# Two halves of a matmul array pass projection groups in two different orders of each triple, 6 turns apart in place of 18

## The chip, the cores and the metric

The kernel runs on one core of a Trainium2 chip. The metric is device time in microseconds (us) from the first to the last work of the core, as the median over runs. The engines of the core work side by side, each on its own list of instructions in order, and wait for one another by semaphores: TensorE (PE, matrix multiplications into PSUM, the accumulator memory of eight banks), VectorE (DVE), ScalarE (ACT), GpSimd (POOL) and SyncE (SP, which here issues every DMA). Times of instructions come from one profiled execution.

## The reference

The output mixes two branches on the same input x (2048 rows of 512) by a gate of one number per row:

```python
g = sigmoid((x * gate_w).sum(-1, keepdims=True))
a = A_ref(x, wqkv, wo)     # 32 heads of 16, causal, window of 256 keys, then @ wo
b = (sigmoid(x @ w_gate) * (x @ w_up)) @ w_down     # F = 1376
return g * a + (1 - g) * b
```

Everything is float32. The kernel makes the products of the projections from a high and a low part of each operand, three products for one: high by high, high by low, low by high.

## The kernel before

**Stages.** A first stage (to about 72 us) projects some q, k and v. Then a loop over steps `u` (`for u in range(N)`, L732; N = 140) runs the attention and, between its pieces, the remaining projections. A last stage multiplies by `w_down` and `wo` and writes the output.

**The attention in the loop.** A step `u` is one group of four heads and one block of 128 rows (8 groups of 16 blocks, 128 steps). Each step has four sub-steps `hh`, one for a head. In each, `s_part(u, hh)` (L305) makes a block of scores on TensorE and DVE takes its row maximum; `st_part(u - LAG, hh ^ 1)` (L353) makes the transposed scores of the step nine earlier, with the maximum built in, and ACT takes the exponent. Both kinds have two PSUM buffers (`"s"` and `"st"`), so a score waits for the maximum, and a transposed score for the exponent, two sub-steps back. After the four heads, POOL masks the block (`mask_p`, L368). At each even `u` TensorE multiplies two masked blocks with v (`pv_part`, L385), and ACT copies the result later (`o_take`, L405). From u=128 (`NU`) there are no scores left, from u=137 no transposed scores.

**Two halves of the array.** Scores and their transposes contract over 64 rows, so a score in the upper half of the array's rows runs beside a transposed score in the lower half. The projections contract over 128 rows and are cut in two to fit in: a *group* is one accumulation of 12 products (`k3 = 3 * ND`) into one PSUM bank; each product is done once by the lower half of the rows (`half` 0) and once by the upper half (`half` 1), both adding into the same bank. Groups are of three kinds: `proj_mm` (q and k, L251; tile `pj`), `gu_mm` (gate and up, L475; tile `gu`), `tail_mm` (the last columns of gate and up, with the gate of the rows, L514; tile `tp`). All three take their banks from tag `"misc"`, which has three, in turn.

**Turns.** `turns()` (L612) is the order of all groups of the loop, `n_rest` = 111 of them: 72 gate/up, 26 projections and 13 of the 16 tails. In turn `t` the lower half does product `t` of the list, the upper half product `t - SHIFT`; with SHIFT = 18 the upper half is a group and a half behind, and always in another bank. A call of `next(slots)` does three turns (`GAP`). The loop calls it after each sub-step: three or four times in a step up to u=127 (the last sub-step of an odd `u` has none), and from u=128 twice after `hh` 1 and twice after `hh` 3. The list of work is `rest` in order of f, then gate or up, then row chunk c; projections are put in `work` at given steps (L765 to L773) and go first.

**What follows a group.** When the upper half has ended a group, its evacuation is put at the head of `acts`; each sub-step takes one entry from `behind` and one from `acts` (L792 to L795), ahead of its turns. For a gate/up group ACT copies the bank to a tile `sp` (four buffers) and the store is issued at the next step (`later`). For a projection ACT copies it (`proj_raw`), then makes the high part (`proj_hi`), and DVE subtracts for the low part (`proj_lo`); at each eighth step `stack_build` (L275) sends two finished projections to the ring that scores read, three DMAs a step. For a tail DVE transposes the bank and copies a column (`tail_post`, L523). When the last row chunk of a gate/up weight is done, `gu_next` (L487) puts the split of the next weight in the same tile.

**The loop's end.** Three tails are held back (`HOLD`): one runs at u=138 with all 128 rows ahead of the last `pv_part`, the other two behind the loop (`hold_group`, L716).

Of the kernel before, what the change touches and what calls it, by code (L numbers as in the profile page):

```python
# [17 lines left out]
ND = D // P  # L18
# [5 lines left out]
NC = T // CH  # L24
NB = T // P
# [3 lines left out]
NFM = NF - 2  # L29
# [9 lines left out]
LAG = 9  # L39
# [2 lines left out]
QB = 32  # L42
HOLD = 3
GAP = 3
SHIFT = 18
TAIL = 109
TREAD = 136
WD_LOAD = {119: 0, 120: 1, 122: 2, 123: 3, 127: 4, 128: 5, 130: 6, 131: 7, 133: 8, 134: 9, 135: 10}
# [7 lines left out]
def gated_mix_kernel(  # L56
# [47 lines left out]
    NSTEP = NG * NC  # L104
# [24 lines left out]
    with ExitStack() as actx:  # L129
# [27 lines left out]
        wq = {}  # L157
# [81 lines left out]
        pj = {}  # L239
# [1 line left out]
        parts = {}  # L241
        stg = {}

        def group_mm(pt, wh, wl, c, k, half):
            d, w = divmod(k, 2) if k < 2 * ND else (k - 2 * ND, 2)
            r = slice(0, P) if half is None else slice(64 * half, 64 * half + 64)
            mm(pt, (wl if w == 2 else wh)[r, d], (xl if w == 1 else xh)[r, d, c * CH:(c + 1) * CH],  # L247
               start=k == 0 and half != 1, stop=k == 3 * ND - 1 and half != 0,
               skip_group_check=half is not None)

        def proj_mm(s, k, half=None):  # L251
            g, c = divmod(s, NC)
            if s not in pj:
                pj[s] = ps.tile([P, CH], F32, tag="misc", name=f"pj{s}", bufs=3)
            group_mm(pj[s], *wq[g], c, k, half)

        def proj_raw(s):
            raws[s] = cpool.tile([P, CH], F32, tag="sp", name=f"pr{s}", bufs=4)
            nc.scalar.copy(raws[s], pj[s])
            pj[s] = raws.pop(s)  # L260

        def proj_hi(s):
            if s % 2 == 0:
                stg[s // 2] = (
                    cpool.tile([P, CH2], F32R, tag="hb", name=f"sh{s}", bufs=4),
                    cpool.tile([P, CH2], F32R, tag="hb", name=f"sl{s}", bufs=4),
                )
# [114 lines left out]
        acts = []  # L382
# [74 lines left out]
        def load_gu(f, w):  # L457
            raw_gu[f, w] = cpool.tile([P, D], F32, tag="draw", name=f"guraw{f}_{w}", bufs=2)
            nc.sync.dma_start(raw_gu[f, w], wgu[f, w])

        gv = w0.rearrange("p l (w d f) -> p l w d f", w=2, d=ND)

        def split_gu(f, w):
            raw = raw_gu.pop((f, w)).rearrange("p (d f) -> p d f", d=ND)
            hi, lo = gv[:, 0, w], gv[:, 1, w]

            def first_half():
                nc.scalar.copy(hi, raw)
                behind.append(lambda: nc.vector.tensor_tensor(lo, raw, hi.bitcast(F32), op=ALU.subtract))

            acts.append(first_half)

        gp = {}

        def gu_mm(f, c, w, k, half=None):  # L475
            if (f, c, w) not in gp:
                gp[f, c, w] = ps.tile([P, CH], F32, tag="misc", name=f"gu{f}_{c}_{w}", bufs=3)
            group_mm(gp[f, c, w], gv[:, 0, w], gv[:, 1, w], c, k, half)

        def gu_post(f, c, w):  # L480
            t = cpool.tile([P, CH], F32, tag="sp", name=f"sp{f}_{c}_{w}", bufs=4)
            nc.scalar.copy(t, gp.pop((f, c, w)))
            later.append((gu_d[w, f, :, c * CH:(c + 1) * CH], t))
            if f + 1 < NFM and c == 0:
                load_gu(f + 1, w)

        def gu_next(f, c, w):  # L487
            if f + 1 < NFM and c == NC - 1:
                split_gu(f + 1, w)

        tw = []
# [19 lines left out]
            nc.scalar.copy(hi, raw)  # L511
            behind.append(lambda: nc.vector.tensor_tensor(lo, raw, hi.bitcast(F32), op=ALU.subtract))

        def tail_mm(b, k, half=None):  # L514
# [4 lines left out]
            mm(tp[b][:, 0:TW], (xl if w == 1 else xh)[r, d, b * P:(b + 1) * P], tw[d][int(w == 2)][r, 0:TW],  # L519
               start=k == 0 and half != 1, stop=k == 3 * ND - 1 and half != 0,  # L520
               skip_group_check=half is not None)

        def tail_post(b):  # L523
            t = cpool.tile([P, CH], F32, tag="sp", name=f"tt{b}", bufs=4)
            nc.vector.transpose(t[:, 0:2 * TF], tp[b][:, 0:2 * TF])
            nc.vector.tensor_copy(gsum[:, b:b + 1], tp.pop(b)[:, 2 * TF:2 * TF + 1])
            later.append((tail_d[b], t[:, 0:2 * TF]))
# [38 lines left out]
        def proj_slot(s, k, half):  # L566
            g, c = divmod(s, NC)
            d, w = divmod(k, 2) if k < 2 * ND else (k - 2 * ND, 2)
            r = slice(64 * half, 64 * half + 64)
            mm(pair_of_banks(f"ph{s}")[half], wq[g][int(w == 2)][r, d], (xl if w == 1 else xh)[r, d, c * CH:(c + 1) * CH],  # L570
               start=k == 0, stop=k == 3 * ND - 1)

        def proj_sum(s):
            lower, upper = halves.pop(f"ph{s}")
            t = cpool.tile([P, CH], F32, tag="sp", name=f"psum{s}", bufs=4)
            nc.scalar.copy(t, lower)
            pj[s] = t
            behind.append(lambda: nc.vector.tensor_tensor(t, upper, t, op=ALU.add))
            soon.append(lambda: proj_post(s))
# [3 lines left out]
        ]  # L583
        rest = [
            (
                lambda k, h=None, a=(f, c, w): gu_mm(*a, k, h),
                lambda a=(f, c, w): gu_next(*a),
                lambda a=(f, c, w): gu_post(*a),
            )
            for f in range(NFM) for w in range(2) for c in range(NC)  # L590
        ] + [
            (lambda k, h=None, b=b: tail_mm(b, k, h), lambda: None, lambda b=b: tail_post(b)) for b in range(NB)
        ]
        work = []
        going = []

        def proj_group(s):
            return lambda k, h=None: proj_mm(s, k, h), lambda: None, lambda: proj_out(s)

        def run_first(n):  # L600
            for _ in range(n):
# [10 lines left out]
        def turns():  # L612
            k3 = 3 * ND
            groups = []
            for t in range(n_rest * k3 + SHIFT):
                if t and t % GAP == 0:
                    yield
                if t % k3 == 0 and len(groups) < n_rest:
                    groups.append((work or rest).pop(0))
                for half, v in enumerate((t, t - SHIFT)):  # L620
                    if 0 <= v < n_rest * k3:
                        groups[v // k3][0](v % k3, half)
                if t >= SHIFT and (t - SHIFT) % k3 == k3 - 1:
                    _, after, post = groups[(t - SHIFT) // k3]
                    acts.insert(0, lambda after=after, post=post: (post(), after()))

        def slot(h, d, c):
            return (xh, xl)[h][:, d, c * CH:(c + 1) * CH]
# [93 lines left out]
        n_rest = len(rest) + NSTEP - 6 - HOLD  # L722
        N = NU + PVLAG + 1
        SUMS = NU - 13 + PVLAG + 1
        U_LAST = 4 * (NSTEP - 2 - 5)
        HLOAD = N - 2 * AHEAD
        done = 0
        slots = turns()
        sdma = []
        wo_raw = []  # L730

        for u in range(N):  # L732
            if u == LAG:
                vctx.close()
# [26 lines left out]
            if u == WO:  # L761
                both = apool.tile([P, ND, CH], F32, tag="w0", name="woraw")
                wo_raw.extend(both[:, d] for d in range(ND))
                nc.sync.dma_start(both, wo.rearrange("(c p) n -> p c n", p=P))
            s4 = {5: 5, 9: 6, U_LAST: NSTEP - 2, U_LAST + 1: NSTEP - 1}.get(u)  # L765
            if u % 4 == 3 and u > LAG and (u + 2) // 4 + 4 < NSTEP - 2:
                s4 = (u + 2) // 4 + 4
            if s4 is not None:
                if u < LAG:
                    first.insert(0, (  # L770
                        lambda k, h, s4=s4: proj_slot(s4, k, h), lambda s4=s4: proj_sum(s4)))
                else:
                    work.append(proj_group(s4))  # L773
# [113 lines left out]
        for n, (c, f) in enumerate(steps):  # L887
# [42 lines left out]
            for t in range(4):  # L930
                b = 4 * c + t
# [60 lines left out]
```

## Time and profile before

| | us |
|---|---|
| median of 3 runs | 745.94 (745.91 to 746.12) |
| span of the profiled execution | 743.8 |
| TensorE busy in it | 737.1 |
| DVE, ACT, POOL busy | 504.5, 432.3, 171.7 |
| loop's first turns / last lone turns | from 72.0 / to 567.3 |

A row of a timeline has the start in us from the span's start, the duration in us, the engine, the line, the operation, output and inputs by the program's names, partitions by columns, and a count where equal rows are merged; in brackets stands idle time of the engine just before, and what ended it. Matmuls are pipelined: the next one starts before the last one has ended, so the cost of one in a row is the distance of the starts. Two rows with nearly the same start are the two halves of the array at work together, and so is a row with the count x2.

### The profile page before, as it was taken

How to read it: one execution, taken by the hardware profiler on the slowest of the kernel's cores; microseconds unless marked ns; L12 is line 12 of the kernel's file. 1: busy time of each engine (PE TensorE's matmuls, PEld its weight loads, DVE VectorE, ACT ScalarE, POOL GpSimd, SP SyncE). 2: the span in 40 equal slices, each digit the busy share in tenths (PEclk: the TensorE clock that was granted, in tenths of full speed). 3: DMA queues.
4: the chain of work that ended last, by engine and by line, in shares of the span. 5: the costliest groups of instructions: out<-in, count | busy, mean ns of one | idle time of the engine just before them, and what ended most of it. 6: DMA issues, size and time to landing. Idle time of an engine off the chain costs nothing.

```text
span 743.8 us, 17724 instructions
## 1 busy us (share of the span) xinstructions
PE 737.1 (99%) x6310; PEld 585.2 (79%) x6310; DVE 504.5 (68%) x1518; ACT 432.3 (58%) x921; POOL 171.7 (23%) x256
## 2 busy tenths in 40 slices
PE   8999999999999999999999999999999999999997
PEld 7888777887777877778787787778777878787886
DVE  5368767766776766776677676677745685848573
ACT  6423676666676667666667666766655573625341
POOL 7000333233233233323323333232331000000000
PEclk9999999999999999999999999999999999999999
DMA  8341434435434453443543426553367878869561
GB/s 302 102 115 34 103 97 118 127 91 160 125 103 119 120 152 109 120 113 110 153 117 99 126 69 174 151 144 116 92 239 206 233 190 212 196 169 227 148 136 58
DMA packets 94321, 103.66 MB, mean 139 GB/s; under 512 B 44926, under 2 KB 57214, under 8 KB 94232
## 3 DMA queue, kind: packets, MB, share of 16 engines
q1 hardware_dynamic: 94232, 102.53, 49.9%
q8 instruction: 49, 0.80, 0.5%
q14 instruction: 40, 0.33, 0.2%
HBM read 45.32 MB, written 31.99 MB: 104 GB/s over the span
## 4 chain that ended last, share of the span: by engine, by line
PE 97%; DVE 1%; DMA 1%; issue 0%; ACT 0%; SPq 0%; POOL 0%; DVEq 0%; POOLq 0%
PE gu L247 28%; PE pv L394 12%; PE pj L247 11%; PE s L315 7%; PE st L361 5%; PE tp L519 5%; PE pd L78 5%; PE pd L80 5%; PE pd L79 5%; PE vh L556 3%; PE pa L78 2%; PE pa L79 2%; PE pa L80 2%; PE vps L79 1%; PE vps L78 1%; PE vps L80 1%
## 5 line engine op out<-in xcount | busy, mean ns | idle before, releaser
L321 DVE CUSTOM_DVE_ANT_0 junk<-s,mask 128x384 f32<-128x384 f32 (+2 forms) x512 | 271.8, 531 | 126.3 <-PE s L315 69.7
L366 ACT ACTIVATE pt<-st 128x384 f32<-128x384 f32 (+2 forms) x512 | 241.6, 474 | 169.9 <-PE st L361 65.3
L247 PE MATMUL gu<-xh,w 64*128 64x512 f32 x1152 | 295.1, 392 | 0.0
L247 PE MATMUL gu<-xl,w 64*128 64x512 f32 x576 | 190.5, 392 | 0.0
L371 POOL TENSOR_SCALAR_AFFINE_SELECT pt<-pt 128x512 f32<-128x512 f32 x128 | 87.7, 685 | 377.2 <-ACT pt L366 377.2
L247 PEld LDWEIGHTS gu<-xh,w 64*128 64x128 f32 x1152 | 160.6, 184 | 14.1
L361 PE MATMUL st<-ring 64*128 64x384 f32 (+2 forms) x536 | 170.1, 332 | 0.2 <-ACT pt L366 0.2
L315 PE MATMUL s<-ring 64*128 64x384 f32 (+2 forms) x536 | 166.6, 329 | 0.4 <-DVE mx L321 0.4
L315 PEld LDWEIGHTS s<-ring 64*128 64x128 f32 x536 | 95.3, 184 | 37.3 <-DVE nm L331 12.5
L361 PEld LDWEIGHTS st<-ring 64*128 64x128 f32 x536 | 97.0, 184 | 11.2 <-issue 2.7
L247 PEld LDWEIGHTS gu<-xl,w 64*128 64x128 f32 x576 | 90.6, 185 | 3.8
L394 PE MATMUL pv<-pt,V 128*32 128x384 f32 (+2 forms) x1408 | 91.0, 388 | 0.0
L247 PE MATMUL pj<-xh,wqh 64*128 64x512 f32 (+1 forms) x228 | 88.6, 395 | 0.4 <-ACT xh L74 0.4
L247 PE MATMUL pj<-xl,wqh 64*128 64x512 f32 (+1 forms) x228 | 88.2, 393 | 0.2 <-DVE xl L75 0.2
L376 POOL TENSOR_SCALAR_AFFINE_SELECT pt<-pt 128x512 f32<-128x512 f32 x112 | 74.4, 664 | 0.0
L247 PE MATMUL pj<-xh,wql 64*128 64x512 f32 (+1 forms) x228 | 69.9, 392 | 0.0
L394 PEld LDWEIGHTS pv<-pt,V 128*32 128x32 f32 x1408 | 37.2, 109 | 35.6 <-issue 29.5
L78 PE MATMUL pd<-ring,hb 128*128 128x512 f32 x160 | 63.0, 394 | 0.0
L80 PE MATMUL pd<-ring,hb 128*128 128x512 f32 x160 | 62.8, 392 | 0.0
L79 PE MATMUL pd<-ring,hb 128*128 128x512 f32 x160 | 62.3, 390 | 0.0
L74 ACT CAST hb<-V 128x512 fp32r<-128x512 f32 x40 | 24.9, 623 | 53.0 <-DVE V L700 51.3
L247 PEld LDWEIGHTS pj<-xh,wqh 64*128 64x128 f32 (+1 forms) x228 | 41.7, 185 | 3.4 <-ACT xh L74 0.9
(122 smaller groups left out, 1145.0 us busy)
## 6 DMA issues: line engine op xcount, KB each, us to landing
gu_scratch<-sp SPq DMA_DIRECT2D x72, 256.0 KB
V<-gu_scratch SPq DMA_DIRECT2D x36, 512.0 KB
ring<-sh SPq DMA_DIRECT2D x128, 128.0 KB
ring<-sl SPq DMA_DIRECT2D x64, 128.0 KB
guraw<-in_wgu_dram SPq DMA_DIRECT2D x18, 256.0 KB
V<-in_xT_dram SPq DMA_DIRECT2D x16, 256.0 KB
oT_scratch<-ob SPq DMA_DIRECT2D x128, 32.0 KB
xl<-oT_scratch SPq DMA_DIRECT2D x16, 256.0 KB
```

The costliest lines, as they stand in the source:

```text
L78: mm(ps, lh, rh, start=first, stop=False)
L79: mm(ps, lh, rl, start=False, stop=False)
L80: mm(ps, ll, rh, start=False, stop=last)
L247: mm(pt, (wl if w == 2 else wh)[r, d], (xl if w == 1 else xh)[r, d, c * CH:(c + 1) * CH], start=k == 0 and half != 1, stop=k == 3 * ND - 1 ...
L315: mm(pt[:, (k - k0) * P:(e - k0) * P], lhsT, blk(g, k, hh, 1, e - k), start=k == k0, stop=e == i + 1, skip_group_check=True,)
L321: nc.vector.tensor_tensor_reduce(junk[:, 0:n], pt[:, 0:n], mask[:, 3 * P - n:], scale=1.0, scalar=NEG, op0=ALU.add, op1=ALU.max, accum_out ...
L361: mm(pt[:, (q - j) * P:(e - j) * P], lhsT, blk(g, q, hh, 0, e - q), start=q == j, stop=e == last, skip_group_check=True,)
L366: nc.scalar.activation(pts[u][:, hh, 0:n], pt[:, 0:n], AF.Exp, scale=SCALE)
L371: nc.gpsimd.affine_select(p[:, :, 0:P], p[:, :, 0:P], pattern=[[0, HG], [1, P]], compare_op=ALU.is_ge, fill=0.0, base=0, channel_multiplie ...
L376: nc.gpsimd.affine_select(p[:, :, 2 * P:], p[:, :, 2 * P:], pattern=[[0, HG], [-1, P]], compare_op=ALU.is_gt, fill=0.0, base=0, channel_mu ...
L394: mm(pv[32 * hh:32 * hh + 32, (q % 4) * P:(q % 4 + e - q) * P], V[:, j, h * VW:h * VW + 32], p[:, hh, (q - j) * P:(e - j) * P], start=Fals ...
L519: mm(tp[b][:, 0:TW], (xl if w == 1 else xh)[r, d, b * P:(b + 1) * P], tw[d][int(w == 2)][r, 0:TW], start=k == 0 and half != 1, stop=k == 3 ...
```

## The change

The upper half goes 6 turns behind the lower one. So that the halves still never work on the same group in the same turn, groups are taken three at a time and the halves pass each triple in different orders: the lower half 0, 2, 1 and the upper half 1, 0, 2 (`TURN`). Which half opens a bank (`start`) and which one closes it (`stop`) now depends on which comes second, and a group's evacuation is queued when both halves have ended it. Since work is taken in threes, projections are put in the list at other steps (`proj_at`), often two at a time. `gu_next` counts a weight's groups instead of looking at c.

```diff
-SHIFT = 18
+SHIFT = 6
+TURN = ((0, 2, 1), (1, 0, 2))
...
-        def group_mm(pt, wh, wl, c, k, half):
+        def group_mm(pt, wh, wl, c, k, half, second):
...
-               start=k == 0 and half != 1, stop=k == 3 * ND - 1 and half != 0,
+               start=k == 0 and not second, stop=k == 3 * ND - 1 and (half is None or second),
...
+        gu_left = {}
+
         def gu_next(f, c, w):
-            if f + 1 < NFM and c == NC - 1:
+            gu_left[f, w] = gu_left.get((f, w), NC) - 1
+            if f + 1 < NFM and gu_left[f, w] == 0:
                 split_gu(f + 1, w)
...
             groups = []
+            halves_done = {}
             for t in range(n_rest * k3 + SHIFT):
                 if t and t % GAP == 0:
                     yield
-                if t % k3 == 0 and len(groups) < n_rest:
-                    groups.append((work or rest).pop(0))
+                if t % (3 * k3) == 0 and len(groups) < n_rest:
+                    groups.extend((work or rest).pop(0) for _ in range(3))
                 for half, v in enumerate((t, t - SHIFT)):
                     if 0 <= v < n_rest * k3:
-                        groups[v // k3][0](v % k3, half)
-                if t >= SHIFT and (t - SHIFT) % k3 == k3 - 1:
-                    _, after, post = groups[(t - SHIFT) // k3]
-                    acts.insert(0, lambda after=after, post=post: (post(), after()))
+                        n, k = divmod(v, k3)
+                        n += TURN[half][n % 3] - n % 3
+                        groups[n][0](k, half, n in halves_done)
+                        if k == k3 - 1:
+                            halves_done[n] = halves_done.get(n, 0) + 1
+                            if halves_done[n] == 2:
+                                _, after, post = groups[n]
+                                acts.insert(0, lambda after=after, post=post: (post(), after()))
...
+        proj_at = {5: [5], LAG: [6, 7], U_LAST: [NSTEP - 2], U_LAST + 1: [NSTEP - 1]}
+        for s in range(8, NSTEP - 2):
+            proj_at.setdefault(4 * s - (20 if s % 2 else 17), []).append(s)
...
-            s4 = {5: 5, 9: 6, U_LAST: NSTEP - 2, U_LAST + 1: NSTEP - 1}.get(u)
-            if u % 4 == 3 and u > LAG and (u + 2) // 4 + 4 < NSTEP - 2:
-                s4 = (u + 2) // 4 + 4
-            if s4 is not None:
+            for s4 in proj_at.get(u, ()):
```

More of the change, by code (lines that the diff above doesn't have):

```diff
@@ L247, in group_mm, with proj_mm @@
             mm(pt, (wl if w == 2 else wh)[r, d], (xl if w == 1 else xh)[r, d, c * CH:(c + 1) * CH],
-               start=k == 0 and half != 1, stop=k == 3 * ND - 1 and half != 0,
+               start=k == 0 and not second, stop=k == 3 * ND - 1 and (half is None or second),
                skip_group_check=half is not None)
-        def proj_mm(s, k, half=None):
+        def proj_mm(s, k, half=None, second=False):
             g, c = divmod(s, NC)
@@ L254, in proj_mm @@
                 pj[s] = ps.tile([P, CH], F32, tag="misc", name=f"pj{s}", bufs=3)
-            group_mm(pj[s], *wq[g], c, k, half)
+            group_mm(pj[s], *wq[g], c, k, half, second)
         def proj_raw(s):
@@ L473, in gated_mix_kernel, with gu_mm @@
         gp = {}
-        def gu_mm(f, c, w, k, half=None):
+        def gu_mm(f, c, w, k, half=None, second=False):
             if (f, c, w) not in gp:
                 gp[f, c, w] = ps.tile([P, CH], F32, tag="misc", name=f"gu{f}_{c}_{w}", bufs=3)
-            group_mm(gp[f, c, w], gv[:, 0, w], gv[:, 1, w], c, k, half)
+            group_mm(gp[f, c, w], gv[:, 0, w], gv[:, 1, w], c, k, half, second)
         def gu_post(f, c, w):
@@ L512, in tail_split, with tail_mm @@
             behind.append(lambda: nc.vector.tensor_tensor(lo, raw, hi.bitcast(F32), op=ALU.subtract))
-        def tail_mm(b, k, half=None):
+        def tail_mm(b, k, half=None, second=False):
             if b not in tp:
@@ L519, in tail_mm @@
             mm(tp[b][:, 0:TW], (xl if w == 1 else xh)[r, d, b * P:(b + 1) * P], tw[d][int(w == 2)][r, 0:TW],
-               start=k == 0 and half != 1, stop=k == 3 * ND - 1 and half != 0,
+               start=k == 0 and not second, stop=k == 3 * ND - 1 and (half is None or second),
                skip_group_check=half is not None)
@@ L585, in gated_mix_kernel @@
             (
-                lambda k, h=None, a=(f, c, w): gu_mm(*a, k, h),
+                lambda k, h=None, x=False, a=(f, c, w): gu_mm(*a, k, h, x),
                 lambda a=(f, c, w): gu_next(*a),
@@ L591, in gated_mix_kernel @@
         ] + [
-            (lambda k, h=None, b=b: tail_mm(b, k, h), lambda: None, lambda b=b: tail_post(b)) for b in range(NB)
+            (lambda k, h=None, x=False, b=b: tail_mm(b, k, h, x), lambda: None, lambda b=b: tail_post(b)) for b in range(NB)
         ]
@@ L597, in proj_group @@
         def proj_group(s):
-            return lambda k, h=None: proj_mm(s, k, h), lambda: None, lambda: proj_out(s)
+            return lambda k, h=None, x=False: proj_mm(s, k, h, x), lambda: None, lambda: proj_out(s)
         def run_first(n):
```

## The prediction

> **What bounds the kernel now.** I read the page first, then busy time by stretches, then TensorE's timeline at the two ends of the loop, and last the other engines beside those ends.
>
> ```profile
> span 743.8 us, 17724 instructions
> ...
> PE 737.1 (99%) x6310; PEld 585.2 (79%) x6310; DVE 504.5 (68%) x1518; ACT 432.3 (58%) x921; POOL 171.7 (23%) x256
> ...
> PE 97%; DVE 1%; DMA 1%; issue 0%; ACT 0%; SPq 0%; POOL 0%; DVEq 0%; POOLq 0%
> ```
>
> TensorE (PE) holds 97% of the chain that ended last. By stretches (columns: length, PE, weight loads, DVE, ACT, POOL busy with counts, granted clock, DMA share, GB/s):
>
> ```profile
> 71.80:78.30 6.50, 6.10 (x36) 4.46 (x35) 5.96 (x20) 4.67 (x10) 1.93 (x2) 1.00 0.60 148
> ...
> 82.00:300.00 218.00, 218.00 (x2269) 169.92 (x2272) 155.50 (x545) 145.47 (x328) 69.92 (x106) 1.00 0.43 118
> ...
> 576.00:700.00 124.00, 124.00 (x546) 100.32 (x546) 85.11 (x152) 60.07 (x104) 0.00 (x0) 1.00 0.76 195
> ```
>
> The loop and the stage behind it leave TensorE no gap. Only the first 6.5 us of the loop do: there DVE works 5.96 us of 6.50. So time can only come from TensorE's own list getting shorter, and can only be lost where TensorE has to wait for a buffer or for another engine.
>
> **The change, part by part.** *Length of the turn list.* The loop works 111 groups of 12 turns (72 gate/up, 26 projections, 13 of the 16 tails). Before, it has 111 x 12 + 18 = 1350 turns, which is 450 calls of three; after, 1338 turns, 446 calls. No matmul is added or removed: 18 turns at each end have one half only before, 6 after. What a turn costs, alone and paired:
>
> ```profile
> 72.00 0.39 PE L247 MATMUL pj<-xh,wqh 64*128 64x512 f32 x1
> 72.02 0.34 PE L315 MATMUL s<-ring 64*128 64x384 f32 x1
> 72.23 0.39 PE L247 MATMUL pj<-xl,wqh 64*128 64x512 f32 x1
> ...
> 75.17 0.44 PE L315 MATMUL s<-ring 64*128 64x384 f32 x1 [0.40 <-DVE mx L321]
> ...
> 84.45 0.33 PE L361 MATMUL st<-ring 64*128 64x384 f32 x1
> ...
> 85.32 0.33 PE L361 MATMUL st<-ring 64*128 64x384 f32 x1
> 85.49 0.40 PE L247 MATMUL gu<-xh,w 64*128 64x512 f32 x2
> 85.72 0.40 PE L247 MATMUL gu<-xl,w 64*128 64x512 f32 x2
> ```
>
> A lone turn starts 0.23 us after the last one (72.00 to 72.23), a pair also 0.23 (85.49 to 85.72). A lone half saves nothing, so twelve turns fewer are twelve full slots fewer. One step hh (a score and a transposed score, then three turns) takes 0.87 us (84.45 to 85.32).
>
> At the loop's start nothing moves: the calls sit at the same steps, with two halves in them from turn 6 on instead of turn 18, and pairs cost what lone turns cost. The wait of 0.40 there is for DVE, and stays. So all of the gain falls at the loop's end, where calls run out four earlier.
>
> *The loop's end.* From turn 1332 on the old loop has the upper half alone: six turns each at step u=135 hh1, u=135 hh3, u=136 hh1. The new one has its lone six at u=135 hh1 and nothing after.
>
> ```profile
> 561.15 0.43 PE L361 MATMUL st<-ring 64*128 64x256 f32 x2
> 561.43 0.36 PE L519 MATMUL tp<-tail_hb,xh 64*128 64x450 f32 x1
> ...
> 562.45 0.37 PE L519 MATMUL tp<-tail_hb,xh 64*128 64x450 f32 x1
> ...
> 562.83 0.38 PE L361 MATMUL st<-ring 64*128 64x256 f32 x1
> 563.05 0.36 PE L519 MATMUL tp<-tail_wqh,xh 64*128 64x450 f32 x1
> ...
> 564.07 0.37 PE L519 MATMUL tp<-tail_wql,xh 64*128 64x450 f32 x1
> 564.37 1.50 PE L394 MATMUL pv<-pt,V 128*32 128x384 f32 x16
> 565.80 0.33 PE L361 MATMUL st<-ring 64*128 64x128 f32 x2
> ...
> 567.26 0.22 PE L361 MATMUL st<-ring 64*128 64x128 f32 x1
> 567.41 0.47 PE L519 MATMUL tp<-tail_wqh,xh 128*128 128x450 f32 x1
> ```
>
> Six tail turns take 1.22 us (five steps from 563.05 to 564.07, 0.204 each). At u=135 the second six vanish: pv follows the score at 562.83 directly, 1.2 us earlier. What pv then waits for is the mask of its last block on POOL and the scores' buffers on ACT:
>
> ```profile
> 561.75 0.63 POOL L376 TENSOR_SCALAR_AFFINE_SELECT pt<-pt 128x512 f32<-128x512 f32 x1
> ```
>
> ```profile
> 562.38 1.25 ACT L366 ACTIVATE pt<-st 128x256 f32<-128x256 f32 x3
> ...
> 566.22 0.28 ACT L366 ACTIVATE pt<-st 128x128 f32<-128x128 f32 x1 [2.59 <-PE st L361]
> 566.45 0.37 ACT L410 COPY ob<-pv 128x256 f32<-128x256 f32 x1
> 566.72 0.28 ACT L366 ACTIVATE pt<-st 128x128 f32<-128x128 f32 x1
> ...
> 571.06 0.37 ACT L410 COPY ob<-pv 128x256 f32<-128x256 f32 x1 [2.62 <-PE pv L394]
> ```
>
> The mask is done at 562.38, pv would start about 563.1: covered. **Gain at u=135: 1.2 us** (1.4 if the last score also comes 0.2 earlier, since a tail's DVE work takes the place of the cast that now holds up the exponents).
>
> At u=136 the cover goes. The four scores use two buffers, so the fourth waits for the second exponent, which ACT runs behind the first and a copy: done at 566.72 + 0.28 = 567.00, 1.20 us behind the first score (565.80). With a wake-up of 0.05 (estimate) and the 0.15 from 567.26 to 567.41, the held tail group starts 1.40 us after that score instead of 1.61. **Gain there: 0.2 us of the 1.22**; bounds 0 and 1.22. In line behind the waiting score stand the held groups and the last pv; ACT's copy at 571.06 follows that pv, and the sigmoids follow the copy, so the last stage moves by as much, still against a full TensorE (124.00 of 124.00). **1.4 us** in both.
>
> *Mixed turns.* Tail 0 starts its lower half at turn 1164 in place of 1176, both with 18 turns mixed with gate/up groups, so six more of the turns cost 0.204 in place of 0.23: **0.2 us**.
>
> *Buffers of the accumulators.* Before, a group holds its bank from turn 12n to 12n+29 and the third next begins at 12n+36: seven turns for the evacuation. After, in a triple from turn T, the groups run T to T+29, T+6 to T+35, T+12 to T+41, and the next in the same banks begin at T+36, T+42, T+48: seven turns again. Ends come at 29, 35, 41 in place of every 12. For gate/up and projections the seven turns cover an ACT copy now and would then. For tails DVE evacuates, and some wait today:
>
> ```profile
> 553.14 0.52 PE L361 MATMUL st<-ring 64*128 64x384 f32 x2
> 553.74 0.44 PE L519 MATMUL tp<-tail_wqh,xh 64*128 64x450 f32 x1
> ```
>
> ```profile
> 553.47 0.12 DVE L526 COPY gsum<-tp 128x1 f32<-128x1 f32 x1
> ```
>
> The matmul waits for the copy that ends at 553.59: about 0.4 us, and everything behind it on TensorE waits too. The tails that hit no pv between their end and the next use wait; walking the turns I count four such before and four after, with different tails. **0**, bounds -0.5 and +1.3 (three more at 0.4).
>
> *Bunched evacuation in the loop.* Two projections now often share a triple, so two casts and two subtractions come within some three steps. DVE has the least room:
>
> ```profile
> 95.55 0.55 DVE L321 CUSTOM_DVE_ANT_0 junk<-s,mask 128x384 f32<-128x384 f32 x1
> ...
> 96.63 0.55 DVE L321 CUSTOM_DVE_ANT_0 junk<-s,mask 128x384 f32<-128x384 f32 x1
> ...
> 97.33 0.56 DVE L321 CUSTOM_DVE_ANT_0 junk<-s,mask 128x384 f32<-128x384 f32 x1
> ```
>
> A maximum takes 0.70 to the next, and 1.08 with a subtraction between, against 0.87 a step: each subtraction puts DVE 0.2 behind and each plain step gives 0.17 back. With two score buffers DVE may lag by about 0.7 us (two steps, 1.74, less the score's 0.34 and the maximum's 0.55, less wake-ups). Two or three subtractions make 0.6. **0**, bounds 0 and +0.4 for each of the 13 pairs.
>
> *Weights and queues.* The gate/up weights of the next f are rewritten once all four groups are done. By my count the shortest room falls from 31 turns to 19 (for f=4 to 5, gate); 19 turns are over six steps, 5 us, for one copy, one cast and one subtraction under 0.7 us each. Projections finish at least three steps u ahead of the DMAs that take them (before at least two), so SP isn't held. Stores come up to two in one u, as already now: the copy below is issued with the next one, 6.4 us on, while its buffer's next use is 42 turns away (48 before), 12 us of steps and pv besides. **0**; an upper bound of 1 us for all three.
>
> ```profile
> 96.63 0.58 ACT L482 COPY sp<-gu 128x512 f32<-128x512 f32 x1
> ```
>
> ```profile
> 103.02 0.85 SPq L289 DMA_DIRECT2D gu_scratch<-sp  x2
> ```
>
> **Sum:** -1.2 - 0.2 (u=135, u=136) - 0.1 (half of the doubtful 0.2) - 0.2 (mixed) = **-1.7 us** of a gross 12 turns (six at 0.23, six at 0.204: 2.6). The profiled span of 743.8 becomes 742.1. The median of the runs, 745.94, lies 2.14 above that span, and nothing here touches what lies around it: **744.2 us**.
>
> **The rivals.** *All twelve turns are had* (0.10): ACT's order at u=136 lets the fourth score through. Against it: the copy at 566.45 stands before the exponent. -2.6: 743.3.
>
> *Given back in pieces* (0.12): the tails' bank waits grow by three (+1.2) or a weight wait appears; -0.5 to +0.5: 745.4 to 746.4.
>
> *DVE falls behind* (0.14), the slower one: place, the steps in which two projections' subtractions meet a gate/up subtraction; the point is a lag over 0.7 us. For it: 155.5 busy of 218.0, more with the bubbles between. Against: the lag as counted stays at 0.6. If 13 pairs cost 0.4 each, +5.2 - 1.7: 749.4.
>
> *The clock drops* (0.02). Every stretch quoted has a granted clock of 1.00; the new wait at u=136 leaves TensorE without work for under 1 us. If it drove the clock to half for the 36 turns of the held groups (7.3 us at 0.204), it would cost up to 7: 751. The Trainium skill ("TensorE: Matmul & The Clock Gate", Part 1) halves the clock only after an idle window of about 3.4 us; by that rule this gap is too short, and no run here yet shows a gap of that length inside the loop.
>
> **Chances and range.** About 0.2% (1.5 us) is what a measurement of this kernel tells from none; the line lies at 744.45. The forecast has 0.62, from 743.3 to 744.9; two thirds of it (0.42) lie below the line, and with the 0.10 of the full gain faster has 0.52. Same: the forecast's other third and the pieces, 0.20 + 0.12 = 0.32. Slower: 0.14 + 0.02 = 0.16. Range 743.2 to 745.6: it leaves out the two slower cases and about a third of the pieces, 0.20 in all.
>
> **What would show it.** Right: the turns list ends one u earlier, the first pv without tails before it comes some 1.2 to 1.4 us sooner, a gap of 0.5 to 1 us before the last score of u=136, ended by ACT; the held groups about 1.7 us earlier, and the stage behind them as long as before. The stretch 82 to 300 still full. Wrong: TensorE's scores waiting for DVE's maximum in the middle of the loop, more than four bank waits among the tails, or the start of the last stage waiting on DMA, so that what the loop gains is lost behind it.

## The result, and the profile after

The changed kernel takes 743.95 us (median of 8 runs, 742.93 to 744.71), the kernel before 745.92 us in the runs beside it (745.19 to 746.25): a ratio of 0.9975, 95% interval 0.9965 to 0.9984. The same kernel measured again gave 744.26 us against 746.03, ratio 0.9975 (0.9967 to 0.9984). Predicted were 744.2 us in a range of 743.2 to 745.6, and both times lie in it. The change is faster by about a quarter of a per cent, just past what such a measurement can tell from nothing.

The spans of the two profiled executions differ by only 0.9 us (743.8 and 742.9). In the one of the changed kernel the first stage, which the change doesn't touch, took 0.68 longer: its first transposed score starts at 72.53, that of the kernel before at 71.85, that of the changed kernel measured again at 71.77, with a span of 742.2. So the stages are compared below by distances, not by spans.

The head of the page of the changed kernel and its chain by engine:

```profile
span 742.9 us, 17744 instructions
...
PE 734.6 (99%) x6310; PEld 580.6 (78%) x6310; DVE 506.6 (68%) x1518; ACT 431.2 (58%) x921; POOL 169.1 (23%) x256
...
PE 93%; DMA 2%; DVE 2%; issue 1%; SPq 1%; ACT 0%; DVEq 0%; ACTq 0%
```

TensorE does the same 6310 matmuls. The chain now holds some DMA, DVE and SP, which end in one short wait, shown below. The kernel's busy time by stretches (columns as in the prediction):

```profile
82.00:300.00 218.00, 218.00 (x2268) 169.16 (x2266) 155.63 (x545) 145.70 (x330) 67.98 (x106) 1.00 0.42 118
576.00:700.00 124.00, 123.90 (x547) 100.36 (x546) 84.72 (x152) 59.63 (x103) 0.00 (x0) 1.00 0.77 194
```

The middle of the loop is as full as before. In the last stage TensorE is idle for a tenth of a microsecond (123.90 of 124.00).

The loop's end on TensorE; these are the rows that answer to 562.83 to 567.41 of the kernel before:

```profile
561.62 0.45 PE L362 MATMUL st<-ring 64*128 64x256 f32 x2
...
562.94 0.36 PE L523 MATMUL tp<-tail_hb,xh 64*128 64x450 f32 x1
563.14 0.28 PE L362 MATMUL st<-ring 64*128 64x256 f32 x1
563.35 1.50 PE L395 MATMUL pv<-pt,V 128*32 128x384 f32 x16
564.78 0.33 PE L362 MATMUL st<-ring 64*128 64x128 f32 x2
565.53 0.32 PE L362 MATMUL st<-ring 64*128 64x128 f32 x1 [0.42 <-ACT pt L367]
566.04 0.32 PE L362 MATMUL st<-ring 64*128 64x128 f32 x1 [0.19 <-ACT pt L367]
566.29 0.47 PE L523 MATMUL tp<-tail_wqh,xh 128*128 128x450 f32 x1
566.60 0.37 PE L523 MATMUL tp<-tail_wqh,xl 128*128 128x450 f32 x1
566.80 0.37 PE L523 MATMUL tp<-tail_wql,xh 128*128 128x450 f32 x1
```

There are no tail products between the last score of u=135 (563.14) and pv (563.35). From the first score of u=135 to that pv it is 1.73 us (561.62 to 563.35); before it was 3.22 (561.15 to 564.37). At u=136 nothing stands between the scores any more, so the third and the fourth wait for an exponent (0.42 and 0.19), and the held tail starts 1.51 us after the first score instead of 1.61.

ACT beside it, with the order exponent, copy, exponent that made the prediction put the fourth score late:

```profile
562.09 0.66 ACT L367 ACTIVATE pt<-st 128x256 f32<-128x256 f32 x2 [0.58 <-PE st L362]
562.63 0.62 ACT L643 CAST xh<-woraw 128x512 fp32r<-128x512 f32 x1
...
565.20 0.28 ACT L367 ACTIVATE pt<-st 128x128 f32<-128x128 f32 x1 [1.17 <-PE st L362]
565.43 0.37 ACT L411 COPY ob<-pv 128x256 f32<-128x256 f32 x1
565.70 0.28 ACT L367 ACTIVATE pt<-st 128x128 f32<-128x128 f32 x1
```

The second exponent ends at 565.98 and the fourth score starts at 566.04. At u=135 both exponents (562.09, x2) now stand ahead of the cast (562.63); before, the cast stood between them.

The table has the distances between starts of TensorE in the profiled execution of each kernel, in us: from the first pv of step u to that of a later u; the whole loop, from its first transposed score to the first product with `w_down`; and the first part of the last stage, from there to the first product with `wo`.

| kernel | u 12 to 120 | 120 to 134 | 134 to 136 | 136 to 138 | loop | last stage, first part | median |
|---|---|---|---|---|---|---|---|
| before | 420.14 | 54.45 | 7.74 | 5.71 | 504.07 | 30.24 | 745.92 |
| changed | 420.11 | 54.30 | 6.24 | 5.62 | 502.26 | 30.58 | 743.95 |
| changed, measured again | 420.17 | 54.30 | 6.23 | 5.62 | 502.35 | 30.50 | 744.26 |
| before, 4 more calls | 424.85 | 54.41 | 6.51 | 5.59 | 507.42 | 30.20 | 749.79 |
| before, new places of projections | 420.12 | 54.43 | 7.74 | 5.71 | 504.01 | 30.22 | 745.76 |
| changed, filled u=136 | 420.08 | 54.29 | 6.23 | 5.25 | 501.86 | 30.52 | 743.92 |
| changed, tails evacuated first | 420.06 | 53.97 | 6.51 | 5.59 | 502.15 | 30.75 | 744.05 |
| changed, reads at u=135 | 420.14 | 54.30 | 6.23 | 5.62 | 502.31 | 34.03 | 745.86 |
| changed, filled, reads at u=135 | 420.46 | 55.47 | 6.23 | 5.25 | 503.42 | 33.96 | 746.54 |
| changed, reads at u=137 | 420.15 | 54.30 | 6.23 | 5.59 | 502.31 | 32.54 | 744.97 |
| changed, filled, reads at u=137 | 420.10 | 54.28 | 6.24 | 5.25 | 501.90 | 30.62 | 744.28 |

The loop is 1.81 us shorter (1.72 when measured again), and 1.50 of that lies in the one stretch from u=134 to 136. From the first product with `wo` to the last product it is 133.36 to 133.40 us in every kernel.

Among the tails' banks the changed kernel waits four times, as counted, at other tails than before. The clearest one, on TensorE and then on DVE:

```profile
515.63 0.33 PE L362 MATMUL st<-ring 64*128 64x384 f32 x1
516.25 0.44 PE L523 MATMUL tp<-tail_wqh,xh 64*128 64x450 f32 x1 [0.29 <-DVE gsum L530]
```

```profile
515.98 0.12 DVE L530 COPY gsum<-tp 128x1 f32<-128x1 f32 x1
```

The new tail may start once the old one's last copy is done (516.10). From the score to the waiting tail product the four take 0.62, 0.36, 0.41 and 0.66 us (2.05 in all); the four of before took 0.47, 0.39, 0.43 and 0.42 (1.71). These are whole distances: a product behind a pair of scores starts 0.17 later where nothing waits (85.32 to 85.49 in the prediction's rows).

At the start of the last stage the changed kernel has a wait that the kernel before doesn't have. Two rows of the chain of waits (start, length, what), the read of the attention's output and the product that waits; then ACT and DVE ahead of that product:

```profile
583.27 6.57 DMA xl<-oT_scratch
...
592.38 0.50 PE pd L81
```

```profile
588.98 0.63 ACT L708 ACTIVATE V<-V 128x512 f32<-128x512 f32 x1 [0.98 <-DMA V<-gu_scratch]
```

```profile
589.64 0.69 DVE L709 TENSOR_TENSOR V<-V 128x512 f32<-128x512 f32 x1 [0.87 <-ACT V L708]
...
590.26 0.73 DVE L881 STREAM_SHUFFLE spare<-xh 128x512 f32<-128x512 f32 x1
...
591.64 0.69 DVE L76 TENSOR_TENSOR hb<-V,hb 128x512 fp32r<-128x512 f32 x1
```

The product starts at 592.38, 0.50 after its predecessor instead of 0.23, once DVE has made the low part for it (591.64). The chain goes back from there to the read of the attention's output. But that read lands at 589.84, and DVE is still busy then: its multiplication of V (589.64) came late, since ACT's sigmoid before it waited for a load of V until 588.98, and the shuffle starts right behind the multiplication. So in this execution it is the load of V that TensorE waits for, by way of ACT and DVE. ACT starts on it 14.2 us after the stage's first product (574.79), against 13.7 in the kernel before (589.64, with the first product at 575.91). When the changed kernel was measured again, ACT starts after 13.8 us (587.95, first product at 574.12) and no product waits there, but from 588 on some 13 us of products stand 0.233 us apart in place of 0.229; the stage's first part is nearly as long.

### The profile page after: what moved, and what is told of

It is laid out like the page before. It is cut to its first block, busy times and chain, and to the rows that moved or that the text cites. A ratio compares the mean times of both kernels' runs of the same rounds, so it can differ in the third digit from the quotient of the medians.

```text
span 742.9 us, 17744 instructions
## 1 busy us (share of the span) xinstructions
PE 734.6 (99%) x6310; PEld 580.6 (78%) x6310; DVE 506.6 (68%) x1518; ACT 431.2 (58%) x921; POOL 169.1 (23%) x256
## 4 chain that ended last, share of the span: by engine, by line
PE 93%; DMA 2%; DVE 2%; issue 1%; SPq 1%; ACT 0%; DVEq 0%; ACTq 0%
PE gu L248 28%; PE pv L395 12%; PE pj L248 11%; PE s L316 7%; PE st L362 5%; PE tp L523 5%; PE pd L81 4%; PE pd L79 4%; PE pd L80 4%; PE vh L560 3%; PE pa L79 2%; PE pa L81 2%; PE pa L80 2%; DMA xl<-oT_scratch 1%; PE vps L79 1%
## 5 line engine op out<-in xcount | busy, mean ns | idle before, releaser
L248 PE MATMUL gu<-xh,w 64*128 64x512 f32 x1152 | 271.0, 393 | 0.0
L248 PE MATMUL gu<-xl,w 64*128 64x512 f32 x576 | 183.0, 392 | 0.0
L372 POOL TENSOR_SCALAR_AFFINE_SELECT pt<-pt 128x512 f32<-128x512 f32 x128 | 86.2, 674 | 378.1 <-ACT pt L367 374.6
L248 PEld LDWEIGHTS gu<-xh,w 64*128 64x128 f32 x1152 | 151.0, 185 | 13.6
L248 PEld LDWEIGHTS gu<-xl,w 64*128 64x128 f32 x576 | 87.7, 185 | 4.0
L248 PE MATMUL pj<-xh,wqh 64*128 64x512 f32 (+1 forms) x228 | 80.1, 394 | 1.1 <-ACT xh L75 1.1
L248 PE MATMUL pj<-xl,wqh 64*128 64x512 f32 (+1 forms) x228 | 80.5, 394 | 0.3
L377 POOL TENSOR_SCALAR_AFFINE_SELECT pt<-pt 128x512 f32<-128x512 f32 x112 | 73.3, 655 | 0.0
L248 PEld LDWEIGHTS pj<-xh,wql 64*128 64x128 f32 (+1 forms) x228 | 41.3, 185 | 3.2
```

The source lines that it names most:

```text
L372: nc.gpsimd.affine_select(p[:, :, 0:P], p[:, :, 0:P], pattern=[[0, HG], [1, P]], compare_op=ALU.is_ge, fill=0.0, base=0, channel_multiplie ...
L377: nc.gpsimd.affine_select(p[:, :, 2 * P:], p[:, :, 2 * P:], pattern=[[0, HG], [-1, P]], compare_op=ALU.is_gt, fill=0.0, base=0, channel_mu ...
```

## The experiments

**Do twelve turns cost the same anywhere? (four more calls in the kernel before)**

```diff
-                if u >= LAG and (hh < HG - 1 or u % 2 == 0 if u < NU else hh % 2 == 1):
+                if u >= LAG and (hh < HG - 1 or u % 2 == 0 or u in (69, 79, 89, 99) if u < NU else hh % 2 == 1):
```

> The kernel before with four more calls of three turns in the middle of its loop (the last sub-steps of u=69, 79, 89, 99), so that its 1350 turns run out at the same sub-step as the changed kernel's 1338. No turn is removed. Theory (the gain is the twelve turns fewer, less what ACT's chain at u=136 takes back): the loop's end looks like the changed kernel's (u=134 to 136 about 1.5 us shorter, u=136 about 0.1), the four steps cost 0.7 each (+2.8), together slower by 0.5 to 1.5 us. Rival (the gain comes from the list ending earlier, wherever the turns go): faster by 1 to 2 us.

Measured: 749.79 us (4 runs) against 745.71; ratio 1.0055 (1.004 to 1.007): slower, by 4.1 us where 0.5 to 1.5 were expected. The end of the loop did nearly what was said (u 134 to 136 shorter by 1.23 in place of 1.5, 136 to 138 by 0.12), and each added call cost 0.69 to 0.71 in its own pair of steps, as said. But each cost 0.47 to 0.49 more in the next pair of steps. TensorE and ACT behind the first of the four:

```profile
312.10 0.33 PE L315 MATMUL s<-ring 64*128 64x384 f32 x1
312.10 0.33 PE L361 MATMUL st<-ring 64*128 64x384 f32 x1
312.65 0.50 PE L247 MATMUL gu<-xh,w 64*128 64x512 f32 x2 [0.23 <-ACT pr L259]
```

```profile
312.02 0.58 ACT L259 COPY pr<-pj 128x512 f32<-128x512 f32 x1
```

A gate/up product waits for the copy of a projection out of the bank that it wants (done at 312.60): the added call has moved all later turns by three against ACT's list. Behind two of the other three calls the trace marks a wait for such an ACT copy too (0.22 us each). The price of a turn stands, and so does the size of what is taken away at the end; that a turn put elsewhere costs a turn and no more does not. Where ACT's copy comes late, the seven turns between two uses of a bank are no spare room.

**The places of the projections alone**

```diff
+        proj_at = {5: [5], LAG: [6, 7], U_LAST: [NSTEP - 2], U_LAST + 1: [NSTEP - 1]}
+        for s in range(8, NSTEP - 2):
+            proj_at.setdefault(4 * s - (20 if s % 2 else 17), []).append(s)
...
-            if s4 is not None:
+            for s4 in proj_at.get(u, ()):
```

> The kernel before with the new steps for the projections alone (often two at a time); order and distance of the halves stay. Theory: nothing is taken off TensorE's list and nothing waits, so each two steps of the loop last as before within 0.05 us and the loop is the same within 0.3 us. Rival (DVE falls behind where two projections' subtractions come together): two-step stretches grow by 0.2 us or more near the pairs, 1 to 5 us in all. Rival (the moved projections bring the gain): faster by 1 us or more.

Measured: 745.76 us (10 runs); ratio 1.0005 (0.9996 to 1.0015). No pair of steps differs from the kernel before by over 0.04 us. Projections two at a time, and the bunching of DVE's subtractions that comes with them at this distance of the halves, cost nothing. In the changed kernel itself, too, no pair of steps up to u=120 differs by over 0.04.

**Is the wait at u=136 worth filling? (five products of the held tail between its scores)**

```diff
-                hold_group(*rest.pop(0))
+                hold_group(*rest.pop(0), range(5, 3 * ND))
...
+                if u == NU + LAG - 1 and hh in (1, 2):
+                    for k in range(3) if hh == 1 else range(3, 5):
+                        rest[0][0](k)
```

> The changed kernel with five of the held tail's twelve products put between the transposed scores of u=136 (three after hh 1, two after hh 2), where TensorE waits for ACT. Theory (ACT's order of exponent, copy, exponent holds TensorE there, and work that is put in is free): the last score of u=136 at most 0.4 us later, the held tail's rest five products (1.0 us) shorter, the last pv 0.5 to 0.9 us earlier from the first score of u=136 on. Rival (TensorE waits for nothing that work could fill, the gap being a drain between array modes): the products cost their full 0.2 us each, no gain.

Measured: 743.92 us (10 runs); ratio 0.9977 (0.9968 to 0.9987): no different from the changed kernel. In the trace u 136 to 138 falls from 5.62 to 5.25, less than the 0.5 expected. TensorE:

```profile
564.17 0.33 PE L362 MATMUL st<-ring 64*128 64x128 f32 x2
564.43 0.48 PE L523 MATMUL tp<-tail_wqh,xh 128*128 128x450 f32 x1
...
564.96 0.36 PE L523 MATMUL tp<-tail_wql,xh 128*128 128x450 f32 x1
565.25 0.32 PE L362 MATMUL st<-ring 64*128 64x128 f32 x1
565.50 0.48 PE L523 MATMUL tp<-tail_wqh,xh 128*128 128x450 f32 x1
```

Nothing waits for ACT now. But a product over 128 rows starts 0.25 after a score over 64 rows, and a score 0.29 after such a product (564.96 to 565.25), where products of one kind stand 0.20 apart (566.60 to 566.80 in the changed kernel). By these distances each change between the two costs about a tenth (an estimate, which leaves a score's own time in), and five products make four more changes.

**The tails' banks (each tail's evacuation ahead of everything else that DVE has to do late)**

```diff
-                                acts.insert(0, lambda after=after, post=post: (post(), after()))
+                                if after is None:
+                                    behind.insert(0, post)
+                                else:
+                                    acts.insert(0, lambda after=after, post=post: (post(), after()))
```

(`after` is None for the tails.)

> The changed kernel with a tail's evacuation by DVE queued at the head of the list of DVE's late work in place of that of ACT's, so ahead of the subtraction or clearing of the same sub-step. Theory (four tails wait for their bank, 0.2 to 0.45 us each beyond the usual step, because DVE's evacuation stands behind other work): two of the four waits go (at u=122 and u=133, 0.4 each), a third shrinks by up to 0.2; stretch from u=120 to u=134 shorter by 0.7 to 1.1 us. Rival (the seven turns of room are too short whatever DVE does): no change there.

Measured: 744.05 us (9 runs); ratio 0.9977 (0.9967 to 0.9987): no different from the changed kernel. The stretch from u=120 to 134 is 0.33 shorter, where 0.7 to 1.1 were expected. The waits at 529.9 and 552.5 went, the one at 516 became another; TensorE and DVE there:

```profile
516.21 0.37 PE L523 MATMUL tp<-tail_wql,xh 64*128 64x450 f32 x1
516.71 0.44 PE L316 MATMUL s<-ring 64*128 64x384 f32 x1
```

```profile
515.10 1.07 DVE L123 TENSOR_TENSOR ring<-wdraw,ring 128x512 fp32r<-128x512 f32 x1
516.10 0.55 DVE L322 CUSTOM_DVE_ANT_0 junk<-s,mask 128x384 f32<-128x384 f32 x1
```

Now the score waits for DVE's maximum, which stands behind a subtraction of 1.07 us: the bank is free sooner, DVE is late for the score. And u 134 to 136 took back 0.27 of the 0.33 won (6.51 against 6.24). ACT's order at u=135 is the old one again:

```profile
560.95 0.38 ACT L367 ACTIVATE pt<-st 128x256 f32<-128x256 f32 x1 [0.56 <-PE st L362]
561.23 0.61 ACT L646 CAST xh<-woraw 128x512 fp32r<-128x512 f32 x1
561.74 1.24 ACT L367 ACTIVATE pt<-st 128x256 f32<-128x256 f32 x3
```

With the cast between the exponents, that stretch is 1.23 us shorter than before, here as in the first experiment; with the cast behind them it is 1.50.

**Reads of the tails one step earlier (`TREAD` 136 to 135)**

```diff
-TREAD = 136
+TREAD = 135
```

> The changed kernel with the small reads of the tails for the last stage begun one step u earlier (end of u=135). Theory (the last stage's start lost 0.3 us because its loads, queued behind these reads, land at nearly the old time while TensorE comes 1.1 us sooner): loop as in the changed kernel within 0.1, from the first product of the last stage to the first product with wo 30.2 to 30.4 us in place of 30.58, as in the kernel before (30.24). Rival (the loss is DVE's or ACT's own work in that stage): 30.5 to 30.7 again.

Measured: 745.86 us (10 runs); ratio 0.9999 (0.9989 to 1.001): all of the gain is gone. The loop is as in the changed kernel, and the first part of the last stage takes 34.03 us in place of 30.58, against the theory. ACT and TensorE there, then TensorE's clock (the 0.50 of the row by stretches):

```profile
588.26 0.63 ACT L708 ACTIVATE V<-V 128x512 f32<-128x512 f32 x1 [5.69 <-DMA V<-gu_scratch]
```

```profile
588.06 0.39 PE L81 MATMUL pd<-ring,hb 128*128 128x512 f32 x1
590.37 0.64 PE L79 MATMUL pd<-ring,hb 128*128 128x512 f32 x1 [1.93 <-ACT hb L75]
590.81 0.63 PE L80 MATMUL pd<-ring,hb 128*128 128x512 f32 x1
```

```profile
591.00:593.80 2.80, 2.80 (x8) 2.16 (x7) 2.77 (x7) 1.82 (x4) 0.00 (x0) 0.50 0.63 205
```

A load of V is late; ACT's sigmoid waits 5.69 us for it (2.74 at the same place in the changed kernel), TensorE 1.93. Behind that wait the granted clock is 0.50 for some 3.4 us, with products 0.44 apart (590.37 to 590.81). The reads stand in SP's queue ahead of that load, which is the first of the two in the last row:

```profile
566.03 3.28 SPq L290 DMA_DIRECT2D xh<-tail_scratch  x3
...
569.89 4.08 SPq L290 DMA_DIRECT2D xh<-tail_scratch  x6
574.07 0.44 SPq L656 DMA_DIRECT2D V<-gu_scratch  x1
...
582.48 0.97 SPq L656 DMA_DIRECT2D V<-gu_scratch  x2
```

Behind the reads SP is 1.4 to 1.5 us later than in the changed kernel: the load at 574.07 is issued there at 572.59, the one at 582.48 at 581.07. ACT starts on the latter at 588.26, in the changed kernel at 585.93.

The profiled execution took 747.48 us. It is one of three of the ten with a mean granted clock of 0.997 (747.48 to 748.21 us); the other seven have 0.999 or 1.000 and took 744.61 to 746.57. So the halved clock doesn't make the median, and no trace shows where the other seven lose their time.

**Both: the filled u=136, reads at u=135**

> The changed kernel with both the products put between the scores of u=136 and the earlier reads. Theory: 0.4 us of the first and 0.2 to 0.3 of the second add up: loop 501.9, last stage's first part 30.2 to 30.4, 0.5 to 0.8 us below the changed kernel. Rival (each gain in the loop is lost at the last stage's start): last stage's first part 30.8 or more, total as the changed kernel.

Measured: 746.54 us (12 runs); ratio 1.0005 (0.9994 to 1.0017). The same loss shows in the trace, 33.96 us for the first part of the last stage, with a gap of 2.28 us between two products and the halved clock behind it. (This execution has another 1.2 us at u=130 and 0.3 at u=90 that the others don't have.) The fill's 0.37 us is there, and lost in it. Here six of the twelve executions have a mean granted clock of 0.997 (747.23 to 748.70 us, the profiled one among them); the other six took 744.88 to 745.86.

**The changed kernel once more**

> The changed kernel once more on the chip of the other two. Theory: ratio 0.997 to 0.998 to the kernel before, the loop 502.3 and the last stage's first part 30.5 to 30.6 again, so that the 0.3 us of loss there isn't chance. Rival (that loss was one execution's): 30.2 to 30.3.

Measured: 744.26 us (10 runs); ratio 0.9975 (0.9967 to 0.9984). The loop's stretches repeat to 0.06 us each. The last stage's first part is again longer than before (30.50), as expected, but this time without the wait.

**Reads one step later (`TREAD` 137), in the changed kernel and in the filled one**

> The changed kernel with the reads of the tails begun one step later (at u=137 in place of 136). In the changed kernel the start of the last stage takes 0.3 us more than before (30.5 to 30.6 against 30.2 from its first product with w_down to its first product with wo). Theory (SP's queue): the tails' reads stand in SP's queue ahead of the load of V and of the reads of the attention's output; begun a step earlier they made it 3.5 us longer, so begun a step later they free the queue earlier: the load of V behind six reads is issued 1 to 3 us earlier (at about 570 instead of 572.6), the wait at the shuffle of the attention's output goes, and the first part of the last stage is 30.2; time 0.3 us below the changed kernel. Rival (the loop's end itself): the wait comes because the last stage now starts 1.7 us earlier and the chain through the last pv, its copy, its store and its read back doesn't start that much earlier; then moving the reads changes less than 0.1 there, time as the changed kernel. Slower case: the reads pushed later are late for the sums of the tails; then the first part is 31 or more.

> The changed kernel with five products of the held tail between the last scores of u=136 and the tails' reads begun one step later. Theory (SP's queue): the loop is 501.9 as with the fill alone, the last stage's first part 30.2 in place of 30.5, and the time 0.5 to 0.8 us below the changed kernel, the best so far. Rival (the loop's end itself): loop 501.9 and the last stage's first part still 30.5 or, since the loop ends another 0.4 earlier, 30.9; time as the changed kernel.

Measured: 744.97 us (11 runs), ratio 0.9989 (0.998 to 0.9997), and 744.28 us (12 runs), ratio 0.9981 (0.9971 to 0.9991). In the first the stage's first part takes 32.54, the slower case (in an execution of 746.02 us, about 1 us above that kernel's median). SP, then TensorE:

```profile
582.21 0.49 SPq L656 DMA_DIRECT2D V<-gu_scratch  x1
582.80 3.05 SPq L290 DMA_DIRECT2D xh<-tail_scratch  x2
585.90 0.49 SPq L873 DMA_DIRECT2D xl<-oT_scratch  x1
```

```profile
588.69 0.50 PE L79 MATMUL pd<-ring,hb 128*128 128x512 f32 x1 [0.26 <-ACT hb L75]
...
592.94 0.50 PE L81 MATMUL pd<-ring,hb 128*128 128x512 f32 x1 [0.44 <-DVE hb L76]
```

The reads that were pushed later now hold up the read of the attention's output: issued at 585.90 here, at 583.27 in the changed kernel. DVE waits 0.32 us for it (to 591.59) ahead of the low part for the product at 592.94. The wait at 588.69 has another source, a load of V on which ACT starts 12.4 us after the stage's first product (586.57, 574.15), in the changed kernel after 11.1. In the filled kernel the first part takes 30.62, not 30.2. So the theory that an earlier or a later place of these reads in SP's queue wins the 0.3 us back falls: both are no better. The rival fits the filled kernel in its milder form, a first part still near 30.5 and the time of the changed kernel; but its condition for the first kernel, under 0.1 of change, isn't met.

## Why the prediction came out

Point by point, in the terms of its sum (changes in us, by the table):

| step of the prediction | predicted | measured |
|---|---|---|
| loop to u=120: lone turns at the start, DVE's bunching, banks, weights, queues | 0 | -0.03 |
| u 120 to 134: mixed turns and the tails' banks | -0.2 and 0 | -0.15 |
| u=135: the six lone turns before pv vanish | -1.2, with -0.1 for half of a doubtful 0.2 | -1.50 |
| u=136: lone turns that had covered a wait | -0.2 | -0.09 |
| last stage to the first product with `wo` | 0 | +0.34, +0.26 |
| from there to the end of the span | 0 | -0.12, -0.11 |
| loop | -1.7 | -1.81, -1.72 |
| loop and last stage | -1.7 | -1.59, -1.57 |

*Where the gain falls* was right: of twelve turns saved, six are had and six turn into the wait for ACT that the order exponent, copy, exponent makes. The rival of all twelve (-2.6) fell with the two waits at u=136 (0.42 and 0.19).

*That the time comes within 0.3 us is in part luck.* The larger gain at u=135 (-1.50 for -1.3) and the loss at the start of the last stage, which the sum puts at nothing, nearly cancel. And the sum adds to the span the 2.14 us of a single execution of the kernel before. In the changed kernel the time lies 1.68 to 1.81 above the span in all eight runs; with 1.7 the sum gives 743.8. By the medians of the spans the change brings 1.5 us when measured again (744.0 to 742.5), where the times give 1.77. The rest lies outside the span, and its cause is open.

*Two sizes were off, in opposite directions.* At u=135 the six turns gave 1.22 of 1.50. The prediction took only half of the 0.2 for the last score; it is 0.27, and what goes with it in every trace is ACT's cast: 1.23 with the cast between the exponents (experiments one and four), 1.50 with the cast behind them. At u=136 the fourth score came 1.26 us after the first, where 1.25 was worked out (1.40 less the 0.15). But the held tail came 0.25 behind it, not the 0.15 read off the row of before. The filled kernel has the same 0.25.

*The tails' banks* cost nothing net, as summed, with the counted four waits; they take 0.34 more by their distances (2.05 against 1.71), so what the prediction calls mixed turns, or something beside them, must have brought about 0.5 in place of its 0.2. The runs don't take these apart. The price of 0.4 for a bank wait was too high: it is the whole distance from the score at 553.32 (the second of the merged row at 553.14) to the product at 553.74. Less the usual 0.17, the wait is about 0.25.

*DVE falls behind* (the slower rival) had 0.14 and is refuted by the second experiment for the bunching, and by the changed kernel's own middle: 420.11 against 420.14 us. *Given back in pieces* has a grain of truth: 0.26 to 0.34 us of the gain is lost at the start of the last stage, as the prediction's list of what would show it wrong names. It is in part the waiting on DMA that stands there. In one execution ACT can start on a load of V only 0.46 later after the stage's first product than in the kernel before: SP issues it only 0.33 earlier (582.73 for 583.06), while the stage starts 1.12 earlier. In the other no product waits, but the products are slightly slower at a granted clock of 1.00, and the cause of that is open. Moving the reads of the tails didn't bring the loss back in either direction. *The clock* stayed at 1.00 through the waits of 0.42 and 0.19: the held products behind them start 0.20 apart (566.60 to 566.80).

What was not tried: other distances of the halves.

No version ran faster than the changed kernel beyond what the runs can tell: the filled one saves 0.40 us of loop in the trace, and its 743.92 us is the changed kernel's 743.95.

## What to carry to other kernels

Work removed from a full engine is worth its time only where nothing else had been hidden under it: go through the removed instructions one by one, and for each ask what it had covered (here ACT's exponents behind six of the twelve). In a list that is full, seven turns between two uses of a buffer can be all in use, so a call added elsewhere may cost more than itself. And a DMA's place in a queue that serves the next stage is to be tried in both directions, with an eye on the stage behind: by the ratios, one step later or earlier cost the changed kernel 1.0 and 1.8 us here, up to all that the change had brought.

## What the hardware showed that was not expected

**Behind a wait of 1.93 us TensorE's clock was halved.** In the kernel with reads at u=135 the granted clock is 0.50 from 591.00 to 593.80, behind a gap of 2.31 us between two starts (588.06 to 590.37), and it recurs behind the gap of 2.28 in the filled one with reads at u=135. Products 0.43 us apart in place of 0.23 added some 1.6 us (8 by 0.2). The Trainium skill ("TensorE: Matmul & The Clock Gate", Part 1) has the clock fall after an idle window of about 3.4 us; by that these gaps were too short. The trace doesn't agree, and the measurement decides: 1.93 us is enough here. It isn't so each time: by their mean granted clock three of ten executions of the one kernel and six of twelve of the other had it. The waits of 0.44 us and under in the other kernels' traces cost no clock, but in one of the ten executions when the changed kernel was measured again, one without a trace, the mean is 0.997 too (745.81 us).

**The two halves of the array seem not to keep the kernel's order between them.** In the rows quoted in the prediction the score at 72.02 starts before the projection products at 72.23, though the kernel's loop issues these products first, in the call ahead of that score: the upper half, which has no product yet, runs ahead. The Trainium skill ("TensorE: Matmul & The Clock Gate", Part 3) says that matmuls start in the order of the program; for halves of the rows this trace doesn't agree, if TensorE's list keeps the kernel's order, which no view shows.
